# Order of the outputs in a two-layer expert kernel: gates of the next token block and the next unit's first step come before a unit's outputs

## The chip, the cores and the metric

The kernel runs on one core of a Trainium2 chip. The metric is device time in microseconds (us), from the start of the program to its end. TensorE (PE) multiplies matrices into PSUM, VectorE (DVE), ScalarE (ACT) and GpSimd (POOL) work on elements, SyncE (SP) starts the loads and stores.

## What is computed

Three stages follow each other on 2 x 768 = 1536 tokens with 512 channels: attention with 8 heads (a window of 128 keys and 4 sink keys), a gated layer with 1536 hidden channels, and a second layer with 2048 hidden channels and a slope per channel for negative values.

```python
def _moe_ref(x, w_gate, w_val, w_out) -> np.ndarray:
    g = x @ w_gate
    silu = g * (1.0 / (1.0 + np.exp(-g)))
    val = x @ w_val
    return (silu * val @ w_out).astype(np.float32)
...
def _moe2_ref(x, w_in, w_out, alpha) -> np.ndarray:
    h = x @ w_in
    g = np.maximum(h, 0.0) + alpha * np.minimum(h, 0.0)
    return (g @ w_out).astype(np.float32)
```

The result is the second layer of the first layer of the attention's output.

## The kernel before, in words

The tokens are handled as three blocks (0, 1, 2) of 512. Every product is made of three matmuls: each operand is split into a high and a low half (`wh`, `wl` for weights, `xh`, `xl` for inputs, `hh`, `hl` for hidden values), and high x high, high x low and low x high are added up. The high half is a rounding copy by ScalarE, the low half a subtraction, on DVE for values (`split_hidden`, L691 to L693) and on POOL for weights (L599).

The weights come as 64-bit numbers and pass through `Stream`: SP loads a tile, ScalarE takes its upper words (L549), DVE puts together the 32-bit number (L584, L587, L590), ScalarE makes `wh` (L593) into one of a few slots that earlier products must have finished reading, POOL makes `wl`. Sums and differences of weight tiles, which a saving form of block products needs, are made by POOL (L567 to L573).

The hidden channels of a layer are cut into units of a few 128-channel tiles. A unit is a Python generator; after each `yield` the driver lets the stream start a further piece of weight work and issues one piece of the list `later` (combinations of inputs for the saving form). The first layer is one unit of `Moe1` for each block (4 hidden tiles) and then four units of `Duo1` (2 hidden tiles each for all three blocks); the second is eight units of `Duo2`. The first and last unit of `Duo1` go block by block (`plain`, L971): two gate products (`ph`, ScalarE's Silu gives `sg`), two value products (`ph`; DVE multiplies by `sg` into `hid`, L966; `split_hidden` gives `hh` and `hl`), and then four output tiles (`po`, L1018 to L1020, six matmuls each), which DVE adds to `acc` (L1023). In the last unit these sums are also split for the second layer (`yh`, `yl`) and combined (L833). The units between use `Chain` (L868): for blocks 0 and 1 seven block products in place of eight (`pa`, `pb`, `pc`, L847), where a copy `u` (L857) of a partial product is taken from PSUM before the bank is added to further, and block 2 by `ph` again; then the outputs of blocks 2, 0 and 1. `Duo2` does the same with one projection and outputs `pf` (L1105 to L1107, summed at L1112); its first unit goes block by block.

All PSUM tiles share one pool of eight banks. The attention's DVE order is fixed by hand. From there on a scheduler lays out each engine's queue: it takes instructions in the order in which the program issues them, as a priority, and follows a simulated timeline; what is issued under `g.soon()` (gates, values, sums) is preferred. An engine then works off its own queue in order, waiting at the head for what the head needs. In both versions TensorE's order is the scheduler's.

## Time and profile before

| | us |
|---|---|
| median of three runs | 673.7 (673.52 to 673.95) |
| the profiled execution | 673.82 |
| its span, first to last instruction | 672.1 |
| TensorE busy | 645.8 (96%), 3032 matmuls |
| weight loads of TensorE busy (beside the matmuls) | 506.1 (75%) |
| DVE / ACT / POOL busy | 473.8 (71%) / 308.7 (46%) / 243.5 (36%) |
| chain of waits that ended last | TensorE 86%, DVE 5%, ACT 4%, POOL 2%, issue 1%, DMA 1% |

The span runs from the first to the last instruction; 1.7 us of the execution lie around it. A group's mean duration counts a matmul as long as its modelled pipeline (0.39 us), though the next one starts 0.23 us after it, so distances between matmuls are read from starts. In a timeline row the number in brackets is the idle time of the engine just before the instruction and what ended it.

### The profile page before, as it was taken

Reading aid. Unit: us, or ns where it says so; the run is one execution under the profiler, and the core shown is the slowest. Engines: PE = TensorE matmul, PEld = TensorE weight load, DVE = VectorE, ACT = ScalarE, POOL = GpSimd, SP = SyncE. Lnnn points to the kernel's source line nnn. Section 1 sums busy time; section 2 is a strip of 40 time slices with the busy share of each in tenths; the row PEclk is TensorE's granted clock in tenths of the full one; section 3 lists DMA queues with packets and bytes.
Section 4 is the critical chain, followed back from the end, with each engine's and each line's share of the span. In section 5 each row is a group of like instructions: output and inputs, shape, how many; then the busy total and the mean of one; then the engine's idle time right before and its main releaser. Section 6 shows DMA issues by size and latency. Waiting matters only on the chain.

```text
span 672.1 us, 8796 instructions
## 1 busy us (share of the span) xinstructions
PE 645.8 (96%) x3032; PEld 506.1 (75%) x3032; DVE 473.8 (71%) x933; ACT 308.7 (46%) x716; POOL 243.5 (36%) x281
## 2 busy tenths in 40 slices
PE   7789899999999899999999989999999999999996
PEld 3457566767788788888878877888888888887885
DVE  6997877353399636678688579848796969686554
ACT  4767856765265214433643335654434252523040
POOL 3547554334113614571334032425344243430000
PEclk8979899999999999999999998999999999999998
DMA  9854444100004203103232111122121213100005
GB/s 273 261 154 144 147 148 134 32 13 1 1 0 130 91 1 93 64 33 126 94 125 95 33 31 62 55 72 63 63 63 63 88 38 95 32 1 0 1 1 192
DMA packets 37205, 52.30 MB, mean 78 GB/s; under 512 B 4385, under 2 KB 28961, under 8 KB 37153
## 3 DMA queue, kind: packets, MB, share of 16 engines
q1 hardware_dynamic: 34944, 51.65, 24.2%
q8 instruction: 26, 0.43, 0.3%
q10 hardware_dynamic: 2208, 0.01, 0.2%
q14 instruction: 27, 0.21, 0.1%
HBM read 48.51 MB, written 3.15 MB: 77 GB/s over the span
## 4 chain that ended last, share of the span: by engine, by line
PE 86%; DVE 5%; ACT 4%; POOL 2%; issue 1%; DMA 1%; SPq 0%; POOLq 0%; ACTq 0%
PE pa L847 9%; PE pf L1105 7%; PE pf L1107 7%; PE pf L1106 7%; PE ph L679 6%; PE ph L680 6%; PE ph L681 6%; PE pb L847 4%; PE po L1018 3%; PE po L1019 3%; PE po L1020 3%; PE xp L321 3%; PE ps_s L225 2%; PE pc L847 2%; PE po L748 2%; PE pg L679 2%
## 5 line engine op out<-in xcount | busy, mean ns | idle before, releaser
L599 POOL TENSOR_TENSOR wl<-w_m,wh 128x512 fp32r<-128x512 f32 x79 | 110.6, 1405 | 197.5 <-ACT wh L593 176.5
L692 ACT ACTIVATE hh<-hid 128x512 fp32r<-128x512 f32 x84 | 52.8, 631 | 83.4 <-DVE hid L966 37.5
L593 ACT ACTIVATE wh<-w_m 128x512 fp32r<-128x512 f32 x68 | 42.9, 631 | 99.3 <-PE pf L1107 40.7
L693 DVE TENSOR_TENSOR hl<-hid,hh 128x512 fp32r<-128x512 f32 x84 | 72.0, 864 | 19.3 <-ACT hh L692 19.2
L1105 PE MATMUL pf<-wh,hh 128*128 128x512 f32 x192 | 75.3, 392 | 0.0
L1106 PE MATMUL pf<-wl,hh 128*128 128x512 f32 x192 | 75.2, 392 | 0.0
L1107 PE MATMUL pf<-wh,hl 128*128 128x512 f32 x192 | 64.7, 392 | 0.0
L584 DVE TENSOR_SCALAR w_m<-w_m 128x512 int32<-128x512 int32 x68 | 35.2, 517 | 37.8 <-ACT w_m L549 37.8
L1112 DVE TENSOR_TENSOR acc<-pf,acc 128x512 f32<-128x512 f32 x84 | 53.3, 683 | 9.8 <-PE pf L1107 9.6
L549 ACT ACTIVATE w_m<-w_raw 128x512 f32<-128x512 f32 x68 | 45.6, 670 | 22.3 <-POOL wl L599 16.6
L587 DVE SCALAR_TENSOR_TENSOR w_m<-w_raw,w_m 128x512 int32<-128x512 int32 x68 | 52.9, 778 | 1.2
L590 DVE SCALAR_TENSOR_TENSOR w_m<-w_raw,w_m 128x512 uint32<-128x512 uint32 x68 | 50.7, 745 | 1.1
L680 PE MATMUL ph<-xl,wh 128*128 128x512 f32 x128 | 49.8, 389 | 0.0
L681 PE MATMUL ph<-xh,wl 128*128 128x512 f32 x128 | 49.8, 389 | 0.0
L679 PE MATMUL ph<-xh,wh 128*128 128x512 f32 x128 | 49.8, 389 | 0.0
L235 ACT ACTIVATE pr<-ps_s,nb 128x160 f32<-128x160 f32 (+2 forms) x96 | 38.0, 406 | 19.5 <-DVE nb L231 17.0
L225 PE MATMUL ps_s<-th 64*128 64x288 f32 (+2 forms) x192 | 39.2, 443 | 7.7 <-ACT pr L235 6.5
L1107 PEld LDWEIGHTS pf<-wh,hl 128*128 128x128 f32 x192 | 36.0, 188 | 8.1
L1018 PE MATMUL po<-hh,wh 128*128 128x512 f32 x96 | 37.8, 394 | 4.5 <-ACT hh L692 4.5
L1106 PEld LDWEIGHTS pf<-wl,hh 128*128 128x128 f32 x192 | 36.0, 188 | 8.1
L1105 PEld LDWEIGHTS pf<-wh,hh 128*128 128x128 f32 x192 | 36.0, 188 | 8.0
L1023 DVE TENSOR_TENSOR acc<-po,acc 128x512 f32<-128x512 f32 x48 | 30.2, 684 | 13.0 <-PE po L1020 13.0
(212 smaller groups left out, 1517.2 us busy)
## 6 DMA issues: line engine op xcount, KB each, us to landing
w_raw<-in_moe_w_out SPq DMA_DIRECT2D x28, 512.0 KB, 3.3
w_raw<-in_moe_w_in SPq DMA_DIRECT2D x16, 512.0 KB, 3.7
w_raw<-in_moe_w_gate SPq DMA_DIRECT2D x12, 512.0 KB, 4.4
w_raw<-in_moe_w_val SPq DMA_DIRECT2D x12, 512.0 KB, 3.6
th<-in_qk SPq DMA_DIRECT2D x16, 336.0 KB, 3.3
vr<-in_v SPq DMA_DIRECT2D x16, 192.0 KB, 2.7
out<-acc SPq DMA_DIRECT2D x12, 256.0 KB, 2.4
th<-in_qk SPq DMA_DIRECT2D x8, 256.0 KB, 5.3
```

The costliest lines, as they stand in the source:

```text
L587: nc.vector.scalar_tensor_tensor(out=mi, in0=sign, scalar=-(2**31), in1=wi, op0=ALU.bitwise_and, op1=ALU.bitwise_or)
L599: eng.tensor_tensor(out=wl, in0=m, in1=wh, op=ALU.subtract)
L679: nc.tensor.matmul(ps, wh[:, c], chan(xh, kk), start=(kk == 0), stop=False)
L680: nc.tensor.matmul(ps, wh[:, c], chan(xl, kk), start=False, stop=False)
L681: nc.tensor.matmul(ps, wl[:, c], chan(xh, kk), start=False, stop=(kk == KD - 1))
L693: nc.vector.tensor_tensor(out=hl, in0=hid, in1=hh, op=ALU.subtract)
L847: self.nc.tensor.matmul(ps, a[:, c], m[:, k], start=(start and k == 0 and y == 0), stop=(k == 1 and y == 2), skip_group_check=True)
L1018: nc.tensor.matmul(ps, wh[:, mc], hh[:, x], start=(x == 0), stop=False)
L1105: nc.tensor.matmul(ps, hh[:, x, ts], wh, start=(x == 0), stop=False)
L1106: nc.tensor.matmul(ps, hh[:, x, ts], wl, start=False, stop=False)
L1107: nc.tensor.matmul(ps, hl[:, x, ts], wh, start=False, stop=(x == DUO - 1))
L1112: nc.vector.tensor_tensor(out=av, in0=ps, in1=av, op=ALU.add)
```

## The change

A unit now yields a marker, `OUT`, before its outputs. The driver holds the unit there, traces the first step of the following unit, then the held outputs, then goes on with the following unit. Pools that were opened and closed between units are now handed over by two callbacks, `lend` and `back`, after the held outputs. Inside `plain`, `first` traces two gate or value products of a block and `second` its outputs, and the order becomes: gates of block 0; for each block its values, the gates of the next block, and then its outputs. The combinations of the first layer's inputs in `later` are issued at every second step in place of every step. The check of the weights' magnitudes, at the end of the weight stream, is cut in two: `decide` (a transpose by TensorE and small DVE operations) is issued `LATE` = 8 steps later.

```diff
--- before.py
+++ after.py
@@ -40,6 +40,8 @@
 VB = 6
 LAG = 2
 SOON = 400
+OUT = "outputs"
+LATE = 8
 ORDER = ((0, 3), (1, 2), (4, 5))
 EARLY = 4
 WARM = 9
@@ -370,8 +372,12 @@
     nc.vector.tensor_reduce(out=red[:, 0:1], in_=ok, axis=AX.X, op=ALU.min)
     one = g.const.tile([P, 1], F32, name="one")
     nc.vector.tensor_reduce(out=one, in_=red, axis=AX.X, op=ALU.min)
+    g.one = one
+
+
+def decide(nc, g):
     ps = g.ps_t.tile([P, 512], F32, tag="ps", name="ps_flag")
-    nc.tensor.transpose(ps[:1, :P], one, g.ident)
+    nc.tensor.transpose(ps[:1, :P], g.one, g.ident)
     fl = g.const.tile([1, 2], F32, name="flag_f")
     nc.vector.tensor_reduce(out=fl[:, 0:1], in_=ps[:1, :P], axis=AX.X, op=ALU.min)
     nc.vector.tensor_scalar(out=fl[:, 1:2], in0=fl[:, 0:1], scalar1=-1.0, scalar2=1.0, op0=ALU.mult, op1=ALU.add)
@@ -734,6 +740,8 @@
                 if last and r == 1:
                     st.done(4)
                 yield
+        if last:
+            yield OUT
         if c == 0:
             self.accs[b] = new_acc(g, "acc1")
         acc, home = self.accs[b]
@@ -970,18 +978,21 @@
 
     def plain(self, w, last):
 
-        pairs = {}
+        pairs, ys = {}, {}
         _, gate, _, value = self.sinks(pairs)
-        for b in range(NPASS):
-            pairs[b] = hidden_pair(self.g)
-            for i, sink in ((0, gate), (DUO, value)):
-                for r in range(DUO):
-                    ps = self.new("ph")
-                    proj(self.nc, ps, self.st.get(w + i + r), *self.xs[b])
-                    sink(b, r, ps, False)
-                    if b == NPASS - 1 and r:
-                        self.st.done(DUO)
-                    yield
+
+        def first(b, i, sink):
+            if i:
+                pairs[b] = hidden_pair(self.g)
+            for r in range(DUO):
+                ps = self.new("ph")
+                proj(self.nc, ps, self.st.get(w + i + r), *self.xs[b])
+                sink(b, r, ps, False)
+                if b == NPASS - 1 and r:
+                    self.st.done(DUO)
+                yield
+
+        def second(b):
             y = [big(self.g, n) for n in ("yh", "yl")] if last else None
             for m in range(KD):
                 self.output(b, m, w + 2 * DUO, *pairs[b], y)
@@ -989,6 +1000,16 @@
             if last:
                 self.accs[b][1][1] += 1
                 self.put(y, self.accs[b][0])
+
+        yield from first(0, 0, gate)
+        for b in range(NPASS):
+            if b < NPASS - 1:
+                yield from first(b, DUO, value)
+                yield from first(b + 1, 0, gate)
+                yield from second(b)
+        yield from first(b, DUO, value)
+        yield OUT
+        yield from second(b)
         self.st.done(DUO)
 
     def unit(self, c):
@@ -1003,6 +1024,7 @@
             chain = self.chain(w + i, self.ops, self.xs[2], room, sink)
             yield from chain.steps(ORDER7)
             chain.done()
+        yield OUT
         for b in (2, 0, 1):
             for m in range(KD):
                 self.output(b, m, w + 4 * DUO, *pairs[b])
@@ -1088,6 +1110,7 @@
                     self.last()
             st.done(DUO)
             w += DUO
+        yield OUT
         for b in (2, 0, 1) if c else range(NPASS):
             yield from self.outputs(c, b, w, *pairs[b])
         st.done(DUO)
@@ -1214,32 +1237,54 @@
     for nm, bufs in (("x_p2", 6), ("u_p", 1), ("h_p2", 1), ("t_p2", 4)):
         setattr(g, nm, ctx.enter_context(tc.tile_pool(name=nm, bufs=bufs)))
     st.idle_pool = True
-    asked = False
-
-    def run(units):
+    asked = 0
+
+    def step():
         nonlocal asked
-        for u in units:
-            for _ in u:
-                if later:
-                    later.pop(0)()
-                st.tick()
-                if not asked and st.n_conv == len(st.seq):
-                    verdict(nc, g)
-                    asked = True
-
-    later.extend(d1.sums())
-    run([m1.unit(0, 2)])
-    assert g.w_ps.pop()[1] == WA
-    early.close()
+        if later:
+            x = later.pop(0)
+            if x:
+                x()
+        st.tick()
+        if st.n_conv == len(st.seq):
+            asked += 1
+            if asked == 1:
+                verdict(nc, g)
+            elif asked == LATE:
+                decide(nc, g)
+
+    inner = ExitStack()
     last = (NF1 - CHUNK) // DUO - 1
-    with ExitStack() as inner:
+
+    def lend():
+        assert g.w_ps.pop()[1] == WA
+        early.close()
         g.x_p3 = inner.enter_context(tc.tile_pool(name="x_p3", bufs=2, side="right"))
-        run([d1.unit(c) for c in range(last)])
+
+    def back():
         assert not later
-    add_pool(nc, tc, ctx, g.w_ps, "w_p3", WA, "right")
-    st.own = range(base - 3 * DUO, len(st.seq))
-    run([d1.unit(last)] + [d2.unit(c, ys) for c in range(NF2 // DUO)])
-    assert asked and not later
+        inner.close()
+        add_pool(nc, tc, ctx, g.w_ps, "w_p3", WA, "right")
+        st.own = range(base - 3 * DUO, len(st.seq))
+
+    later.extend(x for y in d1.sums() for x in (None, y))
+    units = [(m1.unit(0, 2), lend)] + [(d1.unit(c), back if c == last - 1 else None) for c in range(last + 1)]
+    held = None
+    for u, then in units + [(d2.unit(c, ys), None) for c in range(NF2 // DUO)]:
+        for x in u:
+            if x is OUT:
+                break
+            step()
+            if held:
+                for _ in held[0]:
+                    step()
+                if held[1]:
+                    held[1]()
+                held = None
+        held = u, then
+    for _ in u:
+        step()
+    assert asked >= LATE and not later
 
 
 def general(nc, tc, g, q, k, v, w_gate, w_val, w_out, x2_in, x2_out, out):
```

The rows below are from the engines' queues: line, operation, output tile <- input tiles, shape. The number behind a name tells the program's tiles apart; it differs between the two versions.

TensorE in the first unit of `Duo1` ("place 1" in the prediction), before: the two value products of block 0 (`ph_2383`, `ph_2408`, 12 matmuls each) and then the outputs, which read `hh_2327`.

```order
L681 MATMUL ph_2383<-xh_85,wl_2218 128x512
L679 MATMUL ph_2408<-xh_84,wh_2244 128x512
...
L681 MATMUL ph_2408<-xh_85,wl_2245 128x512
L1018 MATMUL po_2431<-hh_2327,wh_2270 128x512
L1019 MATMUL po_2431<-hh_2327,wl_2271 128x512
L1018 MATMUL po_2440<-hh_2327,wh_2270 128x512
...
L679 MATMUL ph_2466<-xh_88,wh_2123 128x512
```

And of the change, where the value products are `ph_2362` and `ph_2388`, the gate products of block 1 `ph_2415` and `ph_2436`:

```order
L687 MATMUL ph_2362<-xh_85,wl_2212 128x512
L685 MATMUL ph_2388<-xh_84,wh_2237 128x512
...
L687 MATMUL ph_2388<-xh_85,wl_2238 128x512
L685 MATMUL ph_2415<-xh_88,wh_2121 128x512
...
L687 MATMUL ph_2415<-xh_89,wl_2122 128x512
L685 MATMUL ph_2436<-xh_88,wh_2147 128x512
...
L687 MATMUL ph_2436<-xh_89,wl_2148 128x512
L1040 MATMUL po_2453<-hh_2360,wh_2265 128x512
L1041 MATMUL po_2453<-hh_2360,wl_2266 128x512
L1042 MATMUL po_2453<-hl_2361,wh_2265 128x512
L1040 MATMUL po_2453<-hh_2360,wh_2290 128x512
```

The 24 matmuls of the next block's gates have moved between the values and the outputs. An output tile now takes its six matmuls in one run, so that the second hidden tile is read by the fourth matmul of the outputs.

DVE at the same place, before: a weight tile's three steps (`w_m_2429`) and the two products `hid` of block 0.

```order
L584 TENSOR_SCALAR w_m_2429<-w_m_2429 128x512
L966 TENSOR_TENSOR hid_2396<-ph_2383,sg_2342 128x512
L587 SCALAR_TENSOR_TENSOR w_m_2429<-w_raw_2305,w_m_2429 128x512
L590 SCALAR_TENSOR_TENSOR w_m_2429<-w_raw_2305,w_m_2429 128x512
L693 TENSOR_TENSOR hl_2328<-hid_2396,hh_2327 128x512
L966 TENSOR_TENSOR hid_2421<-ph_2408,sg_2368 128x512
```

And of the change (L590, L593 and L596 are the weight's steps, L974 is `hid`):

```order
L590 TENSOR_SCALAR w_m_2434<-w_m_2434 128x512
L593 SCALAR_TENSOR_TENSOR w_m_2434<-w_raw_2298,w_m_2434 128x512
L974 TENSOR_TENSOR hid_2375<-ph_2362,sg_2234 128x512
L596 SCALAR_TENSOR_TENSOR w_m_2434<-w_raw_2298,w_m_2434 128x512
L699 TENSOR_TENSOR hl_2361<-hid_2375,hh_2360 128x512
L974 TENSOR_TENSOR hid_2401<-ph_2388,sg_2347 128x512
```

The same six instructions stand there; the first `hid` has moved one instruction back.

TensorE in the last unit of `Duo1` ("place 2"), before: outputs of block 1 (`po_3716` to `po_3746`) inside the second gate product of block 2 (`ph_3780`), then the values (`ph_3803`, `ph_3828`) and the first output of block 2.

```order
L680 MATMUL ph_3780<-xl_94,wh_3234 128x512
L1018 MATMUL po_3716<-hh_3646,wh_3377 128x512
...
L1020 MATMUL po_3746<-hl_3647,wh_3377 128x512
L681 MATMUL ph_3780<-xh_92,wl_3235 128x512
...
L679 MATMUL ph_3803<-xh_92,wh_3252 128x512
...
L679 MATMUL ph_3828<-xh_92,wh_3271 128x512
...
L681 MATMUL ph_3828<-xh_93,wl_3272 128x512
L1018 MATMUL po_3861<-hh_3762,wh_3358 128x512
```

And of the change: outputs of block 1 (`po_3753` to `po_3790`, 24 matmuls), values of block 2 (`ph_3808`, `ph_3826`), the first product of the second layer (`ph_3856`, which reads `yh` and `yl` of block 0), and the first output of block 2.

```order
L687 MATMUL ph_3727<-xh_93,wl_3235 128x512
L1040 MATMUL po_3753<-hh_3676,wh_3365 128x512
...
L1042 MATMUL po_3790<-hl_3677,wh_3384 128x512
L685 MATMUL ph_3808<-xh_92,wh_3252 128x512
...
L685 MATMUL ph_3826<-xh_92,wh_3271 128x512
...
L687 MATMUL ph_3826<-xh_93,wl_3272 128x512
L685 MATMUL ph_3856<-yh_3632,wh_3403 128x512
...
L687 MATMUL ph_3856<-yh_3633,wl_3404 128x512
L1040 MATMUL po_3892<-hh_3806,wh_3365 128x512
```

The gates of block 2 now end before block 1's outputs, and a product of the second layer stands between the values and the outputs of block 2.

DVE at the same place, before, from the first sum of block 1's outputs to the first `hid` of block 2:

```order
L1023 TENSOR_TENSOR acc1_1899<-po_3716,acc1_1899 128x512
L1023 TENSOR_TENSOR acc1_1899<-po_3726,acc1_1899 128x512
L1023 TENSOR_TENSOR acc1_1899<-po_3736,acc1_1899 128x512
L833 TENSOR_TENSOR acc1_1256<-acc1_1899,acc1_1256 128x1024
L693 TENSOR_TENSOR yl_3714<-acc1_1899,yh_3712 128x512
L1023 TENSOR_TENSOR acc1_1899<-po_3746,acc1_1899 128x512
L693 TENSOR_TENSOR yl_3714<-acc1_1899,yh_3712 128x512
L693 TENSOR_TENSOR yl_3715<-acc1_1899,yh_3713 128x512
L693 TENSOR_TENSOR t1l_3757<-acc1_1256,t1h_3756 128x1024
L833 TENSOR_TENSOR acc1_1899<-acc1_1899 128x1024
L693 TENSOR_TENSOR yl_3715<-acc1_1899,yh_3713 128x512
L966 TENSOR_TENSOR hid_3816<-ph_3803,sg_3777 128x512
```

And of the change (L1045 is the sum, L841 the combination, L699 the low half, L974 `hid`):

```order
L1045 TENSOR_TENSOR acc1_1899<-po_3753,acc1_1899 128x512
...
L841 TENSOR_TENSOR acc1_1256<-acc1_1899,acc1_1256 128x1024
L1045 TENSOR_TENSOR acc1_1899<-po_3780,acc1_1899 128x512
L699 TENSOR_TENSOR yl_3751<-acc1_1899,yh_3749 128x512
L590 TENSOR_SCALAR w_m_3850<-w_m_3850 128x512
L1045 TENSOR_TENSOR acc1_1899<-po_3790,acc1_1899 128x512
L699 TENSOR_TENSOR t1l_3801<-acc1_1256,t1h_3800 128x1024
L593 SCALAR_TENSOR_TENSOR w_m_3850<-w_raw_3590,w_m_3850 128x512
L699 TENSOR_TENSOR yl_3752<-acc1_1899,yh_3750 128x512
L841 TENSOR_TENSOR acc1_1899<-acc1_1899 128x1024
L974 TENSOR_TENSOR hid_3821<-ph_3808,sg_3725 128x512
```

Two of a weight's steps (L590, L593) have come in ahead of `hid`, and one low half (`yl_3752`, the second of its tile) has gone behind it.

## Rows read from the trace of the kernel before

**Rows 1.** The page, busy time of each engine.
```profile
PE 645.8 (96%) x3032; PEld 506.1 (75%) x3032; DVE 473.8 (71%) x933; ACT 308.7 (46%) x716; POOL 243.5 (36%) x281
```

**Rows 2.** Windows by stage: stretch, its length, busy time and count by engine.
```profile
369.00:423.00 54.00, 51.46 (x221) 42.04 (x220) 40.05 (x55) 24.57 (x42) 14.62 (x14) 0.97 0.13 40
450.00:606.00 156.00, 156.00 (x684) 128.01 (x682) 127.15 (x194) 61.62 (x116) 64.61 (x60) 1.00 0.19 58
```

**Rows 3.** PE's waits from 180 us on: total, times, longest.
```profile
PE po L1018 <- ACT hh L692: 4.5, 2, 2.5
PE pa L847 <- ACT u L857: 1.1, 2, 0.7
```

**Rows 4.** PE's timeline at place 1: start, duration, instruction, idle and releaser.
```profile
223.62 0.39 PE L681 MATMUL ph<-xh,wl 128*128 128x512 f32 x1
226.00 0.50 PE L1018 MATMUL po<-hh,wh 128*128 128x512 f32 x1 [1.99 <-ACT hh L692]
```

**Rows 5.** DVE's timeline at place 1.
```profile
223.97 0.71 DVE L584 TENSOR_SCALAR w_m<-w_m 128x512 int32<-128x512 int32 x1 [5.43 <-ACT w_m L549]
224.60 0.68 DVE L966 TENSOR_TENSOR hid<-ph,sg 128x512 f32<-128x512 f32 x1
225.20 1.73 DVE L587 SCALAR_TENSOR_TENSOR w_m<-w_raw,w_m 128x512 int32<-128x512 int32 x1
...
229.16 0.68 DVE L966 TENSOR_TENSOR hid<-ph,sg 128x512 f32<-128x512 f32 x1
```

**Rows 6.** ACT's timeline at place 1.
```profile
223.18 0.66 ACT L549 ACTIVATE w_m<-w_raw 128x512 f32<-128x512 f32 x1 [3.00 <-POOL w_m L569]
...
229.87 0.63 ACT L692 ACTIVATE hh<-hid 128x512 fp32r<-128x512 f32 x1 [3.92 <-DVE hid L966]
```

**Rows 7.** POOL's timeline at place 1.
```profile
222.41 0.73 POOL L569 TENSOR_TENSOR w_m<-w_m 128x256 f32<-128x256 f32 x1
```

**Rows 8.** PE's timeline at place 2.
```profile
401.06 0.39 PE L681 MATMUL ph<-xh,wl 128*128 128x512 f32 x1
403.99 0.50 PE L1018 MATMUL po<-hh,wh 128*128 128x512 f32 x1 [2.54 <-ACT hh L692]
...
405.48 0.58 PE L1018 MATMUL po<-hh,wh 128*128 128x512 f32 x1
...
408.85 0.44 PE L679 MATMUL ph<-yh,wh 128*128 128x512 f32 x1
```

**Rows 9.** DVE's timeline at place 2.
```profile
391.97 1.89 DVE L1023 TENSOR_TENSOR acc<-po,acc 128x512 f32<-128x512 f32 x3 [4.72 <-PE po L1020]
393.77 1.22 DVE L833 TENSOR_TENSOR acc<-acc,acc 128x1024 f32<-128x1024 f32 x1
...
396.11 2.60 DVE L693 TENSOR_TENSOR yl<-acc,yh 128x512 fp32r<-128x512 f32 x2
...
399.76 2.31 DVE L833 TENSOR_TENSOR acc<-acc 128x1024 f32<-128x1024 f32 x1
...
402.60 0.68 DVE L966 TENSOR_TENSOR hid<-ph,sg 128x512 f32<-128x512 f32 x1
```

**Rows 10.** POOL's timeline at place 2.
```profile
399.25 1.74 POOL L599 TENSOR_TENSOR wl<-w_m,wh 128x512 fp32r<-128x512 f32 x1 [1.10 <-ACT wh L593]
```

**Rows 11.** PE's timeline at the two short waits.
```profile
340.99 0.40 PE L1020 MATMUL po<-hl,wh 128*128 128x512 f32 x1
341.84 0.50 PE L847 MATMUL pa<-t4h,wh 128*128 128x512 f32 x1 [0.45 <-ACT u L857]
...
605.63 0.39 PE L847 MATMUL pa<-t2h,wl 128*128 128x512 f32 x1
606.70 0.50 PE L847 MATMUL pa<-yh,wh 128*128 128x512 f32 x1 [0.69 <-ACT u L857]
```

**Rows 12.** ACT's waits over the whole span, the first row.
```profile
ACT wh L593 <- PE pf L1107: 40.7, 5, 8.3
```

## The prediction

> **What bounds the kernel now.** I read the page first. TensorE (PE) is busy for 645.8 of the 672.1 us of the span [rows 1]; the next engine stands at 71%. A change of order that adds no matmul can gain only what PE stands idle or runs slowly. Then the windows by stage: from 450 to 606 us PE is busy for the whole 156.00 us, from 369 to 423 us for 51.46 of 54.00 at a mean clock of 0.97 [rows 2]. So the loss sits in a few places. The list of PE's waits after 180 us, where the part that the change touches begins, has only two entries: the output matmuls of the first layer (`po`, L1018) waiting for ScalarE's `hh` twice, 4.5 us, and the chain products (`pa`, L847) waiting for `u` twice, 1.1 us [rows 3]. The attention ahead of 180 us has waits of its own; the order of its instructions is untouched (the first 633 matmuls stand the same), so I count it as unchanged.
>
> Next I priced each place in PE's timeline. A matmul costs 0.2267 us when the next follows at once (start to start; the rows' own durations overlap). What a gap costs is start minus start of the one before, less 0.23.
> - Place 1: 223.62 to 226.00 is 2.38, so 2.15 us lost [rows 4].
> - Place 2: 401.06 to 403.99 is 2.93, so 2.70 us lost. Behind it the clock falls to half: from 405.48 to 408.85 there are 8 matmuls in 3.37 us, where full clock takes 1.81; 1.56 us lost [rows 8].
> - Short ones: 340.99 to 341.84 is 0.62 lost, 605.63 to 606.70 is 0.84 lost [rows 11].
>
> Sum: 2.15 + 2.70 + 1.56 + 0.62 + 0.84 = 7.87 us. That is the ceiling of the gain in this part.
>
> Why place 1 waits: the timeline of DVE shows the `hid` product (L966) at 224.60 directly behind a weight step (L584) that had stood 5.43 us for ScalarE's L549 [rows 5]; L549 at 223.18 had waited 3.00 us for POOL [rows 6], which was still forming the weight sums at 222.41 (L569) [rows 7]. The `hid` itself could have run at about 222: it is queued behind a late weight. Only then come ScalarE's `hh` and PE's `po`. Why place 2 waits: DVE is simply full from 391.97 to 403.28: the last sums of the first layer (L1023), the second layer's input (L693) and its combinations (L833) all stand ahead of one `hid` [rows 9].
>
> **The change part by part.**
> *Plain units (first and last unit of the first layer).* Between a block's two value products and its outputs the two gate products of the next block now stand: 2 x 12 matmuls. In the order of before, `po` of place 1 comes 12 matmuls behind the product that feeds its first `hh`; now it comes 36 behind it, and the second `hh` is wanted 27 behind its own. 24 matmuls are 24 x 0.2267 = 5.4 us of cover against a wait of 2.15. But DVE does not run earlier: its queue holds the same five instructions there, with `hid` one place further back. So I go by the times of before: first `po` now at 223.62 + 25 x 0.2267 = 229.29, first matmul that reads the second `hh` three later, at 229.97. The first `hid` follows L587 (225.20, 1.73 us), so it is done at about 227.6 and its `hh` (0.63 us) at 228.3: in time. The second `hid` comes at 229.16 as before, its `hh` from 229.87 to 230.50 [rows 5, 6]: 0.5 us late, at most 1.3 if the step that is now ahead is held up once more, 0 if POOL's sums come sooner. I take 0.6. The 2.15 become 0.6.
>
> *Holding a unit's outputs behind the next unit's first step.* At place 2 it puts 12 matmuls of the second layer's first product ahead of the last `po`. That product needs only block 0, long done. And since the gates of block 2 come earlier, the outputs of block 1 come as one run of 24, at whose start I set my clock to 0: first `po` wanted at 60 x 0.2267 = 13.6 us. DVE's queue from the first of these sums through `hid`: eight instructions of 128x512 (four sums, three low halves, `hid`) at 1.89/3 = 0.63, three of 128x1024 at 1.22, two weight steps at 0.7: 5.0 + 3.7 + 1.4 = 10.1 [rows 5, 9]. It starts when the first `po` ends (6 matmuls, 1.4) and stands some 0.7 for the second: `hid` ends at 12.2, `hh` at 12.9, 0.7 in time. To this come DVE's stretched instructions. In before L833 took 2.31 at 399.76 instead of 1.22 while POOL's low half of a weight ran from 399.25 for 1.74 [rows 10], and two L693 took 2.60 instead of 1.26: together 2.4 us [rows 9]. POOL's earlier low halves hang on slots that the gates of block 2 free, and these now end before the outputs start; the one that hangs on a value product's slot (product ends at 36 x 0.2267 = 8.2) still falls into the run. One stretch of 1.09 gives `hh` at 14.0, 0.4 late; none gives 0; all of 2.4 gives 1.7. I take 0.4. PE's 1.99 us of idle at place 1 was followed by full clock, the 2.54 at place 2 by half [rows 4, 8], so after 0.4 I expect no fall: 1.56 gained too.
>
> The Trainium skill, page "SBUF — State Buffer", section "Who interferes with whom", says that a VectorE instruction with two SBUF inputs and a GpSimd instruction that reads SBUF exclude each other, the later one standing until the first ends. By that rule the L833 of [rows 9] would end at 400.99 + 1.22, so last 2.45; the trace has 2.31, which agrees. It speaks against the change wherever a POOL low half slides into DVE's run at place 2: that is rival B below.
>
> *Short waits.* The chain product that reads `t4` stood one matmul behind the one that frees its `u`, now at least 12; the pair at 605.63 stands 18 or more apart. 12 matmuls are 2.7 us against waits of 0.62 and 0.84: gone. Any new order can leave a wait of that kind: 0 to 1.5 (both of them again); I take 0.2, near none, since no pair that near stands in the new order.
>
> *Pacing and the deferred flag.* The weight sums of the first layer are started one in two steps. In POOL's queue they keep their places, SP's loads keep their order: 0, bounded by -0.5 and +0.5 (a POOL sum is 0.73 [rows 7], and PE had no wait on a weight). The flag's transpose and reduction are issued 8 steps later, one matmul and small operations; the last 84 matmuls keep their order, so the tail is the same: 0. The pools change hands with the same banks; the nearest reuse of a PSUM bank goes from 18 matmuls to 23, so no wait there.
>
> Sum: 7.87 - 0.6 - 0.4 - 0.2 = 6.7 us gained. The profiled execution took 673.82 (span 672.1, 1.7 around it), which gives 667.1; the median of the three runs, 673.7, lies 0.1 below it, hence **667.0 us**.
>
> **The rivals.**
> *B: the waits only shrink.* POOL's low halves go on colliding with DVE at both places: 1.3 stays at place 1, 1.7 at place 2, and that idle is again followed by half clock (1.56; between the 1.99 that was not and the 2.54 that was, nothing decides it). Gain 7.87 - 1.3 - 1.7 - 1.56 - 0.2 = 3.1: 670.6. For it: in before DVE lost 2.4 us this way at the same place. Against: two of the three weights come earlier.
>
> *C: the wait moves.* The work that DVE must do for the second layer is the same; what `hid` no longer waits for, the sums behind it may. If a sum that empties a PSUM bank comes late, PE stands at the following products for the same 4 to 8 us: 673.7. My count of DVE's queue behind `hid` leaves about 1 us there, so it needs more than two stretched instructions in a row.
>
> *D: slower.* ScalarE's weight copies (L593) stood 40.7 us, in 5 cases, for second-layer outputs to free a slot, up to 8.3 each, with whatever is queued behind them [rows 12]. The first product of the next unit now goes in front of those outputs: at least 6 matmuls, 1.36 us, at 11 unit boundaries from there on. If an `hh` or `u` that PE soon wants stands behind the copy, each boundary costs those 1.36: 15.0 - 7.87 = 7.1 slower, 680.8. It decides as soon as the reader of such an `hh` comes within some 10 matmuls of the copy's release; against it, in the new order the readers stand 66 or more matmuls from the product that feeds them.
>
> **How the numbers follow.** The forecast gets 0.67, B 0.15, C 0.09, D 0.09. The forecast's own span is 665.3 (nothing left over, and 0.5 from the pacing) to 668.5 (its residues doubled); B reaches to 670.6. Range 665.0 to 671.0, which leaves C and D out, 0.18 together. A measurement of this kernel can tell about 0.2%, 1.35 us, from no change: forecast and B are faster by more, 0.82; C within, 0.09; D slower, 0.09.
>
> **What would show it.** Right: in PE's waits after 180 us no entry `po` <- `hh` over 1 us; full clock from 385 to 425 us; PE above 97%. In DVE's timeline at place 1 the `hid` still behind a weight step that waits for L549's successor: the cover grew, the delay did not shrink. B: a residual `po` <- `hh` of over 1 us with a DVE instruction of over 2 us ahead of it and a POOL low half beside it, and a stretch of half clock. C: a new row of PE waiting for a sum (`acc`) to free its bank. D: more than 41 us of L593's successor waiting for `pf`, and `pa` or `pf` waiting behind it. Wrong altogether if PE loses no less than 7 us after 180 us.

## The result and the profile after

The changed kernel takes 667.3 us (median; 666.41 to 667.7 in 4 runs) against 673.75 of before (4 runs): a ratio of 0.9902, 95% interval 0.9885 to 0.9920, so 6.4 us or 1.0% faster. The forecast was 667.0. The profiled execution is the fastest of the four: 666.41, span 664.7. In the series further down some executions of before lie at 677 to 678.5 us; the ratios there count them, so differences are given between medians.

TensorE's share rises by a point, to 97.0% (644.7 of 664.7), which is at the forecast's mark of "above 97%" and not over it; its busy time hardly changes, since the work is the same. The page, busy time of each engine, answering to [rows 1]:

```profile
PE 644.7 (97%) x3032; PEld 506.3 (76%) x3032; DVE 484.5 (73%) x933; ACT 309.3 (47%) x716; POOL 249.3 (38%) x281
```

The window around place 2 (columns as in [rows 2], then the granted clock, the DMA share and GB/s):

```profile
369.00:423.00 54.00, 54.00 (x239) 44.54 (x238) 41.71 (x57) 27.85 (x48) 15.66 (x12) 1.00 0.12 40
```

From 369 to 423 us PE is now busy throughout at a granted clock of 1.00, where it had stood 2.54 us and run at 0.97. The list of PE's waits after 180 us, which had two rows of 4.5 and 1.1 us [rows 3], has one:

```profile
PE po L1040 <- ACT hh L698: 0.2, 1, 0.2
```

Place 1 in three timelines of the changed kernel. PE, where [rows 4] had 1.99 us of idle:

```profile
229.76 0.39 PE L1040 MATMUL po<-hh,wh 128*128 128x512 f32 x1
...
230.22 0.39 PE L1042 MATMUL po<-hl,wh 128*128 128x512 f32 x1
230.81 0.50 PE L1040 MATMUL po<-hh,wh 128*128 128x512 f32 x1 [0.20 <-ACT hh L698]
231.15 0.39 PE L1041 MATMUL po<-hh,wl 128*128 128x512 f32 x1
231.53 0.50 PE L1042 MATMUL po<-hl,wh 128*128 128x512 f32 x1
```

DVE, answering to [rows 5]:

```profile
224.35 0.71 DVE L590 TENSOR_SCALAR w_m<-w_m 128x512 int32<-128x512 int32 x1 [4.44 <-ACT w_m L555]
225.10 0.98 DVE L593 SCALAR_TENSOR_TENSOR w_m<-w_raw,w_m 128x512 int32<-128x512 int32 x1
226.01 0.68 DVE L974 TENSOR_TENSOR hid<-ph,sg 128x512 f32<-128x512 f32 x1
...
229.41 0.68 DVE L974 TENSOR_TENSOR hid<-ph,sg 128x512 f32<-128x512 f32 x1
```

ACT, answering to [rows 6]:

```profile
223.56 0.67 ACT L555 ACTIVATE w_m<-w_raw 128x512 f32<-128x512 f32 x1 [1.95 <-POOL w_m L575]
...
226.72 0.63 ACT L698 ACTIVATE hh<-hid 128x512 fp32r<-128x512 f32 x1 [2.40 <-DVE hid L974]
230.12 0.63 ACT L698 ACTIVATE hh<-hid 128x512 fp32r<-128x512 f32 x1 [2.77 <-DVE hid L974]
```

The weight step still stands at the head of DVE's queue for 4.44 us and holds up `hid` (L974), and the two `hh` start at 226.72 and 230.12 where before had 225.31 and 229.87. Counted from the start of the last value product's last matmul (224.10 here, 223.62 before), the first is 0.93 us later than in before and the second only 0.23 earlier. What has changed is that PE has 24 matmuls to do meanwhile. The first `hh` is there 2.4 us before its reader, the second 0.37 us after the time at which PE would have read it (229.76 + 3 x 0.2267 = 230.44).

Place 2, on four engines of the changed kernel: DVE, POOL, ACT and PE.

```profile
390.06 0.69 DVE L1045 TENSOR_TENSOR acc<-po,acc 128x512 f32<-128x512 f32 x1 [4.71 <-PE po L1042]
...
397.03 0.69 DVE L593 SCALAR_TENSOR_TENSOR w_m<-w_raw,w_m 128x512 int32<-128x512 int32 x1
397.63 0.69 DVE L699 TENSOR_TENSOR yl<-acc,yh 128x512 fp32r<-128x512 f32 x1
398.23 1.23 DVE L841 TENSOR_TENSOR acc<-acc 128x1024 f32<-128x1024 f32 x1
399.37 0.69 DVE L974 TENSOR_TENSOR hid<-ph,sg 128x512 f32<-128x512 f32 x1
```

```profile
397.35 3.27 POOL L605 TENSOR_TENSOR wl<-w_m,wh 128x512 fp32r<-128x512 f32 x1 [6.86 <-ACT wh L599]
```

```profile
400.64 0.67 ACT L555 ACTIVATE w_m<-w_raw 128x512 f32<-128x512 f32 x1 [3.38 <-POOL wl L605]
...
401.31 0.62 ACT L698 ACTIVATE hh<-hid 128x512 fp32r<-128x512 f32 x1
```

```profile
402.11 0.40 PE L1040 MATMUL po<-hh,wh 128*128 128x512 f32 x1
```

DVE comes to `hid` after 9.3 us (390.06 to 399.37), where it took 10.6 in before (391.97 to 402.60, [rows 9]): none of its instructions is stretched in this run. POOL's low half is, 3.27 us in place of 1.3 to 1.7. That delays ScalarE's L555, which waits for POOL and stands ahead of `hh` in ScalarE's queue: `hid` ends at 400.06, `hh` starts only at 401.31 and ends at 401.93, 0.18 us before PE reads it without a wait. The second trace of the same kernel, further down, has the stretch on DVE and not on POOL, and no wait either.

### The profile page after: what moved, and what is told of

The parts are those of the page before. It is cut to its first block, busy times and chain, and to the rows that moved or that the text cites. A ratio compares the mean times of both kernels' runs of the same rounds, so it can differ in the third digit from the quotient of the medians.

```text
span 664.7 us, 8778 instructions
## 1 busy us (share of the span) xinstructions
PE 644.7 (97%) x3032; PEld 506.3 (76%) x3032; DVE 484.5 (73%) x933; ACT 309.3 (47%) x716; POOL 249.3 (38%) x281
## 4 chain that ended last, share of the span: by engine, by line
PE 82%; DVE 9%; ACT 4%; issue 2%; POOL 2%; DMA 1%; SPq 0%; POOLq 0%; ACTq 0%
PE pa L855 9%; PE pf L1129 7%; PE pf L1128 7%; PE pf L1130 7%; PE ph L687 6%; PE ph L686 6%; PE ph L685 6%; PE pb L855 5%; PE po L1040 3%; PE po L1042 3%; PE po L1041 3%; PE ps_s L227 3%; PE xp L323 2%; PE pc L855 2%; PE ps_p L282 2%
## 5 line engine op out<-in xcount | busy, mean ns | idle before, releaser
L605 POOL TENSOR_TENSOR wl<-w_m,wh 128x512 fp32r<-128x512 f32 x79 | 115.0, 1460 | 215.6 <-ACT wh L599 200.1
L699 DVE TENSOR_TENSOR hl<-hid,hh 128x512 fp32r<-128x512 f32 x84 | 71.1, 855 | 17.4 <-ACT hh L698 16.8
L1130 PE MATMUL pf<-wh,hl 128*128 128x512 f32 x192 | 70.5, 392 | 0.0
L555 ACT ACTIVATE w_m<-w_raw 128x512 f32<-128x512 f32 x68 | 45.7, 672 | 33.5 <-POOL wl L605 23.9
L596 DVE SCALAR_TENSOR_TENSOR w_m<-w_raw,w_m 128x512 uint32<-128x512 uint32 x68 | 60.3, 887 | 1.2
L593 DVE SCALAR_TENSOR_TENSOR w_m<-w_raw,w_m 128x512 int32<-128x512 int32 x68 | 52.2, 768 | 1.3
L590 DVE TENSOR_SCALAR w_m<-w_m 128x512 int32<-128x512 int32 x68 | 37.1, 545 | 20.4 <-ACT w_m L555 19.8
L1045 DVE TENSOR_TENSOR acc<-po,acc 128x512 f32<-128x512 f32 x48 | 31.6, 683 | 15.8 <-PE po L1042 15.8
```

The lines of the kernel that those rows point to most:

```text
L596: nc.vector.scalar_tensor_tensor(out=mu, in0=lo.bitcast(U32), scalar=29, in1=mu, op0=ALU.logical_shift_right, op1=ALU.bitwise_or)
L605: eng.tensor_tensor(out=wl, in0=m, in1=wh, op=ALU.subtract)
L699: nc.vector.tensor_tensor(out=hl, in0=hid, in1=hh, op=ALU.subtract)
L1130: nc.tensor.matmul(ps, hl[:, x, ts], wh, start=False, stop=(x == DUO - 1))
```

## The experiments

All but the last were timed in series with the kernel before on the same chip; each ratio is against those runs. Pacing and flag were run together, on the kernel before. In that trace POOL's instructions stand in the same order from the first to the last, and those of PE, DVE and ACT up to 604 us, shortly ahead of the flag's transpose (608 us in before). So nothing is seen of the pacing, and what "pacing and flag" shows below is put down to the flag. The changed kernel with the old pacing was not run.

| kernel | median us | before us | ratio (95% interval) |
|---|---|---|---|
| old order in the plain units (changed kernel else) | 671.38 | 674.23 | 0.9946 (0.9922 to 0.9971) |
| no holding (changed kernel else) | 672.27 | 674.23 | 0.9962 (0.9943 to 0.9981) |
| pacing and flag alone | 672.87 | 674.23 | 0.9972 (0.9955 to 0.9989) |
| two steps held | 666.41 | 674.23 | 0.9879 (0.9853 to 0.9905) |
| before, third weight buffer | 672.05 | 673.60 | 0.9974 (0.9958 to 0.9990) |
| before, combinations on POOL | 674.90 | 673.60 | 1.0022 (1.0006 to 1.0037) |
| changed kernel again | 667.18 | 673.60 | 0.9901 (0.9880 to 0.9922) |
| two steps held, again | 666.24 | 673.60 | 0.9882 (0.9860 to 0.9904) |
| changed kernel, flag not late | 667.35 | 673.48 | 0.9904 (0.9887 to 0.9921) |

**The old order in the plain units.** Only `plain` is undone.

```diff
-        yield from first(0, 0, gate)
         for b in range(NPASS):
...
+            yield from first(b, 0, gate)
+            yield from first(b, DUO, value)
+            if b == NPASS - 1:
+                yield OUT
+            yield from second(b)
```

> The changed kernel with plain units in the old order (gates, values, outputs of each block in turn); holding the last outputs behind the next unit's first step, the pacing and the late flag stay. Theory (each wait is closed by matmuls put between a value product and its reader): the wait at the first plain unit comes back, 2 us, since nothing stands between block 0's values and its outputs; at the last plain unit block 2's outputs stay held, so no long wait and no half clock there; the two short waits stay gone. 673.75 - 7.9 + 2.2 = 668.0 by that sum, 669.5 when compared with the changed kernel's 667.3. Rival (the gain is the holding's alone): 667.3, no wait over 0.5 us in the first plain unit. Rival (the gain is the new order's in the plain units alone): 673.7.

PE's timeline of this kernel, at place 1 and in the first unit of the second layer:

```profile
224.86 0.39 PE L687 MATMUL ph<-xh,wl 128*128 128x512 f32 x1
228.20 0.50 PE L1037 MATMUL po<-hh,wh 128*128 128x512 f32 x1 [2.95 <-ACT hh L698]
...
230.74 0.63 PE L685 MATMUL ph<-xh,wh 128*128 128x512 f32 x1
231.16 0.63 PE L686 MATMUL ph<-xl,wh 128*128 128x512 f32 x1
...
421.64 0.73 PE L685 MATMUL ph<-yh,wh 128*128 128x512 f32 x2 [0.76 <-ACT yh L698]
```

And DVE at place 1:

```profile
225.16 0.71 DVE L590 TENSOR_SCALAR w_m<-w_m 128x512 int32<-128x512 int32 x1 [4.44 <-ACT w_m L555]
225.91 0.98 DVE L593 SCALAR_TENSOR_TENSOR w_m<-w_raw,w_m 128x512 int32<-128x512 int32 x1
226.81 0.68 DVE L974 TENSOR_TENSOR hid<-ph,sg 128x512 f32<-128x512 f32 x1
```

The wait is back, and larger than the 2 us expected: 2.95, because DVE's `hid` now stands one weight step further back than in before [rows 5], without the cover that made up for it. Half clock followed (in the rows from 230.74 on matmuls come 0.43 us apart), and a new short wait of 0.76 came up. No entry at place 2. The time, 671.38, is 1.9 us above the 669.5 of the theory, which had neither the longer wait nor the half clock nor the new wait. So both rivals that credit one part alone are out: 2.9 of the 6.4 us remain.

**No holding.** The driver ignores the marker.

```diff
-            if x is OUT:
-                break
-            step()
-            if held:
...
+            if x is not OUT:
+                step()
...
```

> The changed kernel without holding: every unit's outputs are traced before the next unit's first step; the new order inside the plain units, pacing and late flag stay. Theory: the first plain unit stays without a long wait; at the last plain unit block 2's values come straight before its outputs again, so the wait of 2 to 3 us comes back and half clock after it (1.6 us more); the short chain waits (0.6 and 0.8) come back in part: 667.3 + 2.7 + 1.6 + 0.8 = 672.4, between 670 and 673. Rival (holding is not needed, the earlier gates and the outputs in one run already free the last plain unit): 667.3 to 668.

PE's waits of this kernel, and then DVE and POOL at place 2:

```profile
PE po L1040 <- ACT hh L698: 2.8, 2, 2.3
PE pa L855 <- ACT u L865: 0.5, 1, 0.5
```

```profile
397.76 0.69 DVE L593 SCALAR_TENSOR_TENSOR w_m<-w_raw,w_m 128x512 int32<-128x512 int32 x1
398.36 1.78 DVE L699 TENSOR_TENSOR yl<-acc,yh 128x512 fp32r<-128x512 f32 x1
...
401.20 0.68 DVE L974 TENSOR_TENSOR hid<-ph,sg 128x512 f32<-128x512 f32 x1
```

```profile
398.08 1.52 POOL L605 TENSOR_TENSOR wl<-w_m,wh 128x512 fp32r<-128x512 f32 x1 [6.87 <-ACT wh L599]
```

Place 2 is back with 2.33 us and half clock behind it, the time is as the theory had it (672.3 of 672.4). Of the two short waits the one at 341 us is back, the one at 606 us isn't. DVE's and POOL's instructions stand here in the order of the changed kernel. But in this run it is DVE's `yl` that stood, 1.78 us against 0.69 in the changed kernel's first trace, where POOL took 3.27. The starts don't tell which of the two engines pays: in both traces POOL's low half starts 0.32 us after DVE's L593 and 0.28 before `yl`. It also falls out both ways in two executions of one and the same kernel (the second trace of the changed kernel, below).

**Pacing and flag alone, on the kernel before.**

```diff
+LATE = 8
...
+                if st.n_conv == len(st.seq):
+                    asked += 1
+                    if asked == 1:
+                        verdict(nc, g)
+                    elif asked == LATE:
+                        decide(nc, g)
...
+    later.extend(x for y in d1.sums() for x in (None, y))
...
```

> The kernel before with only the pacing of the first layer's sums and the late flag. Theory: neither touches a wait of TensorE, so 673.7, within 0.5, with the same four waits. Rival (the sums no longer compete with the weight steps on VectorE, so the first plain unit's wait shrinks): 671.6 to 673, with a wait under 1.5 us there.

```profile
PE po L1023 <- ACT hh L697: 4.5, 2, 2.5
PE pa L852 <- ACT u L862: 0.5, 1, 0.5
```

Expected no difference; measured 1.4 us faster (interval 0.7 to 3.0), and not by the rival either, which looked at place 1. PE's waits show where: `pa` has one entry of 0.5 in place of two of 1.1. The wait at 606 us [rows 11] is gone, because without the flag's transpose among the chain products the scheduler sets other products between the one that frees `u` and its reader. In this trace half clock is also missing after the 2.54 us at place 2. From the last value product of `Moe1` to the last matmul it is 461.30 us, against 462.20 in the trace of before in which the clock stayed up there (the last experiment): 0.9 us, about what the wait and the matmul behind it lost.

**Two steps held.**

```diff
+        n = 0
...
-            if held:
+            n += 1
+            if held and n == 2:
```

> The changed kernel holding a unit's outputs behind the next unit's first two steps instead of one. Theory: no wait of TensorE over 0.3 us is left after the first plain unit, so more cover brings nothing: 667.3, within 0.5. Rival D of the prediction (each matmul put in front of the outputs holds ScalarE's weight copies and what is queued behind them): slower by up to 1.36 us at each of 11 boundaries, up to 15 us, seen as ScalarE's weight copies waiting for pf well over 34 us and chain products or outputs waiting behind them.

The rival D has nothing for it: no entry at all in PE's waits after 180 us, and the kernel is no slower. The theory's 667.3 was missed the other way: 666.41, 0.9 us below it. It was timed again beside the one-step version:

> The changed kernel holding two steps, beside the one-step version on the same chip. Theory: the only loss that the one-step version has left is the first plain unit's, some 0.7 us with what follows it, which the two-step version did not show: 0.3 to 1.0 us faster than the one-step version. Rival: no difference, within 0.3.

666.24 (664.69 to 666.70) against 667.18 (666.60 to 667.51) in the same series: 0.9 us, the size of what place 1 still lost (0.37 in front of the matmul, and 0.37 in the three behind it). The two intervals against before overlap, but the traces agree: from the last value product of `Moe1` to the last matmul it is 455.15 us in both traces with two steps and 455.96 and 455.91 in the two with one. At place 1 DVE's first `hid` now stands ahead of the weight step and waits for its own product alone, and the second `hh` ends at 230.50, 1.06 us before its reader.

**The cause at place 1: a weight tile in a buffer of its own, on the kernel before.**

```diff
-        m = g.raw_w.tile([P, KD * P], F32, tag="m", name="w_m")
+        m = (g.m3 if hasattr(g, "m3") and not g.exact and i == 19 else g.raw_w).tile([P, KD * P], F32, tag="m", name="w_m")
...
-    for nm, bufs in (("x_p2", 6), ("u_p", 1), ("h_p2", 1), ("t_p2", 4)):
+    for nm, bufs in (("x_p2", 6), ("u_p", 1), ("h_p2", 1), ("t_p2", 4), ("m3", 1)):
```

> The kernel before, with one weight tile (the second of the pair whose sums POOL forms at the first plain unit) in a buffer of its own, so that ScalarE's L549 of the weight queued ahead of the first hid no longer waits for POOL's sums; the order on TensorE is as before. Theory: the wait at the first plain unit is the hid behind that late weight in DVE's queue; with the weight early, hid runs when its product is there (about 221.5 us in the times of before), hh at 222.8, ahead of the 223.85 at which po wants it: the 2 us entry goes, nothing else: 674.2 - 2.15 = 672.1; the last plain unit keeps its 2.5 us. Rival (12 matmuls between product and reader are simply too few): the wait of 2 us stays, 674.2.

DVE and PE at place 1 of this kernel:

```profile
221.01 1.11 DVE L590 SCALAR_TENSOR_TENSOR w_m<-w_raw,w_m 128x512 uint32<-128x512 uint32 x1
223.24 0.69 DVE L966 TENSOR_TENSOR hid<-ph,sg 128x512 f32<-128x512 f32 x1 [1.11 <-PE ph L681]
```

```profile
225.46 0.39 PE L681 MATMUL ph<-xh,wl 128*128 128x512 f32 x1
225.69 0.39 PE L1018 MATMUL po<-hh,wh 128*128 128x512 f32 x1
```

`hid` now waits for its own product and for nothing else ([1.11 <-PE ph]), and `po` follows the last value product at 0.23 us. Only the weight's buffer was changed; the order on PE is the old one, 12 matmuls between product and reader. So the cause was the late weight at the head of DVE's queue, and the change covers it without removing it. Time 672.05, 1.6 less than before, with an interval of 0.7 to 2.8 us that holds the 2.15 of the theory. In the traces, from the last value product of `Moe1` to the last matmul, it is 2.18 us (460.02 against the 462.20 of before with the clock up).

**The cause at place 2: combinations on POOL, on the kernel before.**

```diff
+    def pool_sub(self, out, x, y):
+        return lambda: self.nc.gpsimd.tensor_tensor(out=out, in0=x, in1=y, op=ALU.subtract)
...
         self.last = self.split(c, t3)
+        self.add, self.sub = self.pool_add, self.pool_sub
```

> The kernel before, with the four sums and differences that combine the first layer's result for the second (L833) on POOL instead of DVE; all else as before. Theory: the wait at the last plain unit is DVE being full; two L833 (1.13 and 2.23 us start to start) leave the queue ahead of hid, hid ends 3.4 us earlier and hh is there before po wants it: the 2.5 us entry goes, and the half clock behind it where there was one: 674.2 - 2.7 - 0 to 1.6 = 670 to 671.5. Rival (the lock between DVE and POOL only moves): POOL's 1024-wide sums stretch DVE's low halves instead, the wait shrinks by less than 1.5 us: 673 or more.

DVE, POOL and PE of this kernel at place 2:

```profile
394.99 2.58 DVE L693 TENSOR_TENSOR yl<-acc,yh 128x512 fp32r<-128x512 f32 x1
...
398.09 4.09 DVE L693 TENSOR_TENSOR yl<-acc,yh 128x512 fp32r<-128x512 f32 x3
402.11 2.29 DVE L693 TENSOR_TENSOR t1l<-acc,t1h 128x1024 fp32r<-128x1024 f32 x1
404.32 0.68 DVE L972 TENSOR_TENSOR hid<-ph,sg 128x512 f32<-128x512 f32 x1
```

```profile
394.62 2.40 POOL L836 TENSOR_TENSOR acc<-acc,acc 128x1024 f32<-128x1024 f32 x1 [1.00 <-ACT yh L692]
...
398.92 2.72 POOL L836 TENSOR_TENSOR acc<-acc 128x1024 f32<-128x1024 f32 x1 [0.87 <-DVE yl L693]
```

```profile
405.78 0.50 PE L1024 MATMUL po<-hh,wh 128*128 128x512 f32 x1 [3.10 <-ACT hh L692]
```

The theory failed and its rival came out: 1.3 us slower than before, and the wait grew from 2.54 to 3.10. POOL took 2.40 and 2.72 us for sums that cost DVE 1.2, and DVE stood meanwhile: 2.58 for one `yl` of 0.69, 4.09 for three, 2.29 for `t1l` of 1.21. Work moved from DVE to POOL did not leave DVE's way. That DVE's run ahead of `hid` sets the wait is still borne out, since it lengthened with that run; that emptying DVE would remove the wait was not shown by this. Nor does any run take away the two stretched instructions, which made up 2.4 us of that run in before [rows 9], with all else as it was; how much of the wait is theirs and how much the plain amount of work is open.

**The changed kernel again, and with the flag at once.**

> The changed kernel once more, for a second trace and to be timed beside the next one. Theory: 667.3 as before; what differs between its runs is the length of the half-clock stretches in the attention, since the part after 200 us has no wait over 0.5 us. Rival: the spread comes from the last plain unit, where hh was ready only 0.16 us before its reader: then a wait of up to 1 us shows there in this trace.

The second trace has the same single wait of 0.20 and none at place 2. But what happened there differs from the first trace. DVE, POOL, ACT and PE:

```profile
398.28 1.78 DVE L699 TENSOR_TENSOR yl<-acc,yh 128x512 fp32r<-128x512 f32 x1
...
401.12 0.68 DVE L974 TENSOR_TENSOR hid<-ph,sg 128x512 f32<-128x512 f32 x1
```

```profile
397.99 1.52 POOL L605 TENSOR_TENSOR wl<-w_m,wh 128x512 fp32r<-128x512 f32 x1 [6.86 <-ACT wh L599]
```

```profile
401.83 0.63 ACT L698 ACTIVATE hh<-hid 128x512 fp32r<-128x512 f32 x1 [1.52 <-DVE hid L974]
```

```profile
402.74 0.39 PE L1040 MATMUL po<-hh,wh 128*128 128x512 f32 x1
```

Here DVE's `yl` was stretched and POOL's low half wasn't, and `hh` waits for `hid` alone. DVE comes to `hid` after 10.4 us (390.70 to 401.12), where the first trace had 9.3, and `hh` ends at 402.46, 0.28 us before its reader. The kernel without holding has the same 10.4 us on DVE (390.79 to 401.20) and a wait of 2.33. So what closes the wait is the 12 matmuls that stand ahead of the reader here and not there.

The rival, a wait of up to 1 us at place 2, is out. The last value product of the first layer's first unit starts at 202.99 us here, at 202.34 in the first trace; from there to the last matmul it is 455.91 and 455.96 us. The spread between executions lies in the attention, in front of everything that the change touches.

```diff
             if asked == 1:
                 verdict(nc, g)
-            elif asked == LATE:
                 decide(nc, g)
```

> The changed kernel with the flag's transpose and reduction issued at once instead of 8 steps later; order of the outputs and holding stay. Theory (the short wait near the end of the weight stream comes from the flag: with it at once, the scheduler sets the next chain product of pa straight behind the product whose copy u it needs): the 0.7 us entry of pa waiting for u comes back near 600 us, 0.84 lost, 667.2 + 0.8 = 668.0. Rival (holding has already put those products apart): 667.2, no such entry.

667.35, no entry of `u`: the rival is right. From the last value product of `Moe1` to the last matmul it is 456.05 us, 0.1 from the traces with the late flag. The late flag is worth something on the kernel before, and nothing that these runs can tell once outputs are held; either of them puts the two products apart.

**The kernel before again.**

> The kernel before once more, for a second trace. Theory (whether half clock follows an idle of 2 to 3 us differs between executions): the 2.54 us of idle at the last plain unit are there, and the stretch of half clock behind them may be missing, with the part from 200 us on then 1.6 us shorter than in the first trace. Rival (half clock always follows that idle in this kernel): the stretch is there again.

The window from 404 to 412 us in the two traces of before, the first and then this one (length, busy time and count by engine, granted clock, DMA share, GB/s):

```profile
404.00:412.00 8.00, 8.00 (x28) 6.42 (x29) 8.00 (x12) 3.84 (x5) 0.23 (x1) 0.79 0.06 14
```

```profile
404.00:412.00 8.00, 6.19 (x27) 5.15 (x28) 8.00 (x12) 3.85 (x5) 0.00 (x0) 1.00 0.00 0
```

The same 2.54 us of idle stands ahead of the matmul at 405.81 in this one, and the clock stays at 1.00. The part from the last value product of `Moe1` to the last matmul is 462.20 us, against 463.87: 1.7 less, as the theory had it. Half clock after that wait is not the kernel's doing alone: of the four traces with this same wait (before twice, pacing and flag, third buffer) one has it. This execution is no faster for it (674.07 against 673.82): its attention ended 1.85 us later (last value product at 203.71, in the first trace at 201.86).

## Why the prediction was right, and where not

*The ceiling.* 7.87 us were counted for four places. The same sum over the changed kernel's trace leaves 0.37 at place 1 and 0.37 in the three matmuls behind it. From the last value product of `Moe1` to the last matmul it is 463.87 us in the first trace of before and 455.96 after: 7.9 less. The mechanism (matmuls put between a value product and its reader, and a clock that stays up) is the one forecast. The other trace of before, in which the clock stayed up by itself, has 462.20, so 6.2 less after.

*Place 1, residue 0.6.* 0.37 and as much again in the matmuls behind it, as each of them still ran up to its operands. The second `hid` came at 229.41 where 229.16 was worked out, in a trace that runs 0.48 us later at this place: 0.2 us sooner than worked out. The statement that the cover grows and the delay doesn't shrink holds, and the third buffer shows its cause.

*Place 2, residue 0.4.* None, by 0.18 us in the first trace and 0.28 in the second. DVE's run was mis-sized: from its first sum to `hid` the working gives 10.2 us without a stretched instruction and 11.3 with one; the traces have 9.3 and 10.4. The working added up durations (0.63, 1.22 and 0.7 us), but the rows overlap: from start to start it is 0.60 for 128x512, 1.14 for 128x1024, and 0.3 and 0.6 for the two weight steps. That 0.9 us is why even the one stretch, which was to make `hh` 0.4 late, left it in time. In the first trace, where the exclusion fell on POOL, `hh` was held elsewhere: in ScalarE's queue behind a weight step that waited for the POOL instruction so stretched. The working looked at DVE's queue alone.

*Half clock, 1.56.* This term was mis-sized. It came from one execution; three other traces with the same 2.54 us wait don't have it. Its mean over the four is 0.4, not 1.56. The forecast counted it in full on the ground that half clock had followed 2.54 us of idle; the same idle in the same kernel didn't bring it a second time. The waits alone are 2.15 + 2.70 + 0.62 + 0.84 = 6.31; what is left at place 1 takes 0.7 of it, 0.4 comes from the matmuls just behind each wait (0.11 each), and 0.4 from the clock: 6.4, the measured difference of the medians. That the sum came out only 0.3 from it is in part luck: errors that cancel, a clock term too large by 1.2 and residues too large by about 0.5, and the small rest behind the waits that was not counted.

*The short waits, 0.2.* Both are gone. What does it for the one at 606 was put down to the holding; the late flag does it as well. The one at 341 comes back without holding, with the flag late.

*Pacing and flag, 0.* Pacing: nothing is seen of it, as forecast. Flag: in the step that costed it at nothing, on the ground that it is one matmul and a few small operations, its place in the schedule was overlooked. Alone it is worth 1.4 us by the medians (0.7 to 3.0) and 0.9 in the traces, of which 0.84 is the wait. In the whole change it adds nothing that was measured (667.35 without, 667.18 and 667.3 with, in three series). Of the last 84 matmuls that were to keep their order only the last 47 do in the traces; the tail is as long as it was, 6.4 us from the last matmul's start to the end of the span in both.

*Parts together.* By the medians the order alone (with the flag) gains 2.0 us, the holding alone (with the flag) 2.9, the whole 6.4. Each part alone keeps one of the two long waits, as its trace shows, and in that trace a half-clock stretch behind it.

*The rivals.* B: the exclusion that the Trainium skill's page "SBUF — State Buffer" gives in "Who interferes with whom" agrees with the traces of place 2. B needed it to fall on DVE. In the changed kernel it fell on POOL in the first trace (3.27 us for 1.3) and on DVE in the second (1.78 for 0.69), and no wait followed there either: what B described happened in part, what it was to cost did not. That the later one stands until the first ends can't be read from the rows, whose starts are alike in both traces. C: no wait for a bank. D: ScalarE's copies wait less than in [rows 12], and two held steps cost nothing. ACT's waits of the changed kernel:

```profile
ACT wh L599 <- PE pf L1130: 33.9, 5, 8.7
```

*The spread.* The upper end of the forecast's own span, 668.5, is 0.3 above what its own words give (residues doubled: 667.0 + 1.2 = 668.2). Nothing hangs on it.

## What to carry to other kernels

Price an engine's stall at the reader: count what the busy engine can do between the product and its first reader, and compare it with the longest chain through the other queues, all of them, including the one that only copies. Add up such a chain from starts and not from durations: here the durations made it 0.9 us too long. A term that rests on a clock stretch seen in one execution is worth a part of itself until a second trace shows it. When outputs can be held behind independent work, one step more than the worked-out need is worth a trial: here it cost nothing and took away the residue that was left.

## What the runs showed of the hardware

Whether half clock (1.2 in place of 2.4 GHz) follows an idle of TensorE between full stretches differs between executions: it came after 2.54 us in one of four traces, two of them of the same kernel. After about 2 us (1.97 to 2.03) it came in none of four traces; the one trace each with 2.33 and 2.95 us has it, the one with 3.10 doesn't. The attention, whose matmuls stand in the same order in all kernels, ends between 200.97 us (two steps held) and 203.71 us (before again) by the start of the last value product behind it, with half-clock stretches of different length (over the first 84 us the mean granted clock is 0.94 in the former and 0.88 in the latter); that is more than the spread of any kernel's part behind it.

DVE's two-input instructions and POOL's subtraction exclude each other in both directions: POOL's 128x512 subtraction takes 1.3 us alone, and took 3.27 while DVE ran three of them on end; DVE's 128x512 subtraction takes 0.69 alone, and took 1.78 beside that subtraction of POOL's and 2.58 beside a 128x1024 sum on POOL. Which of the two stands is not told by the starts in the rows: six traces have the same order at place 2, with POOL's start 0.31 to 0.32 us after DVE's L593, and POOL stood in two of them (the changed kernel's first, two steps held) and DVE in four (the changed kernel's second, flag at once, two steps again, no holding).
